# Five weight and cache loads of a two-layer decode kernel, split into DMAs of 112, 8 and 8 rows

## The chip, the cores and the metric

The kernel runs on one core of a Trainium2 chip. The metric is the device time of one execution in microseconds (us). Before the change it is 2562.59 us, the median of 3 runs (2562.34 to 2562.93).

The core has five engines with instruction streams of their own: TensorE (PE, with its weight loads as PEld), VectorE (DVE), ScalarE (ACT), GpSimd (POOL) and SyncE (SP). Here SP issues every transfer between device memory (HBM) and the on-chip memory (SBUF, 128 partitions). A transfer is carried out by up to sixteen DMA engines at once, each with a queue of its own, and each adds one to the transfer's semaphore when its part has landed.

## The reference

Two layers, each a cached attention block followed by an MLP block, for a batch of 2 and one new token. All inputs are bfloat16.

```python
def _A_ref(x, k_cache, v_cache, wq, wo):          # B=2, Sq=1, D=576, H=32, Sk=16384, Dh=128
    q = (x @ wq).reshape(B, Sq, H, Dh).transpose(0, 2, 1, 3)
    scores = jnp.einsum("bhqd,bhkd->bhqk", q, k_cache) * (Dh ** -0.5)
    p = _softmax(scores, axis=-1)
    o = jnp.einsum("bhqk,bhkd->bhqd", p, v_cache)
    return o.transpose(0, 2, 1, 3).reshape(B, Sq, H * Dh) @ wo

def _B_ref(x, w1, w2, w3, w4):                    # w1, w2: 576x576, w3: 576x4608, w4: 4608x576
    h = _gelu(_layernorm(x) @ w1)
    ...
    x1 = x + jnp.concatenate([g0, g1, g2, g3], axis=-1) @ w2    # shifted quarters of h
    return x1 + _gelu(_layernorm(x1) @ w3) @ w4

x = A_x
for _ in range(2):
    x = x + _A_ref(_layernorm(x), A_k_cache, A_v_cache, A_wq, A_wo)
    x = x + _B_ref(_layernorm(x), B_w1, B_w2, B_w3, B_w4)
```

Both layers read the same caches and weights. With 64 pairs of batch and head, one layer reads 64 K tiles and 64 V tiles of 16384x128 numbers, 4 MB each. (A few tiles at the border of the layers are kept and read once.)

## The kernel before

**Memory and order of loads.** One SBUF tensor, `mem`, has six slots of 32768 bytes in each partition. A K or V tile fills one slot: partition p holds 128 cache rows one behind another, so that a tile is a DMA of 128 rows of 32768 bytes. Weights go into parts of the same slots. `plan_all` lists every load of the whole program once, in the order of issue, with its place: `plan_tile` and `plan_piece` (L421, L429) list K and V tiles, `plan_cols` (L434) lists wq and w3, cut by 128 of their 576 rows into four loads of 128 rows and one of the 64 rows that are left (as 128 half rows), `plan_rows` lists wo and w4 (rows of 1152 bytes), and `plan_small` w1 and w2. A 128-row load of w3 has rows of 9216 bytes.

**The queue.** `Store.pump` (L286) takes the list from the front: a load is issued as soon as every cell of its place is free, and a load that has to wait holds up all that come behind it. `Graph.dma` (L91) makes one SP operation of a planned load: it may consist of several DMAs ("starts"), all of which add 16 to one semaphore, and a user waits for the sum. `release` frees a place when its last user is done.

**Compute.** `attention` (L769) goes over the 64 pairs. For each K tile, PE transposes half of it (L963), ACT copies the transposes out (L974), PE makes scores from them (L985), and DVE computes the other half of the scores by multiplying and reducing (L1007, L1011). After a softmax (L1018 to L1037) PE multiplies with the V tile (L1067). Between the layers, and at the end, come the projections: wo, two LayerNorms, w3 (`z_projection`, L736), gelu, and w4 (`rows_projection`, L715); then, for layer 1, wq. While these run, the first transposes of layer 1 are already made (`ahead`), and at the end of the kernel the same projections are followed by the store of the result.

**Names.** In both layers the loads behind the last V tile are, in the order of the queue: wo in pieces, then (layer 1 alone) w1, then w3 as five loads and w4 in pieces. In layer 0 wq of layer 1 and the rest of a K tile follow. w1 of layer 1 is a DMA of 4x128 rows, one of 56 rows and one of 8 rows.

Of the kernel before, what the change touches and what calls it, by code (L numbers as in the profile page):

```python
# [327 lines left out]
class KB:  # L328
# [89 lines left out]
        self.mps = ps("mps", [128, 512], FP32)  # L418


    def plan_tile(self, t, u, slot, cuts=()):  # L421

        b, hh = u % self.B, u // self.B
        src = (self.K if t == "k" else self.V)[b, hh].rearrange("(p j) d -> p (j d)", p=128)
        cuts = [0, *cuts, self.NB]
        for a, z in zip(cuts[:-1], cuts[1:]):
            self.plan_piece(t, u, slot, src, a, z - a)

    def plan_piece(self, t, u, slot, src, a, n):  # L429
        sem = f"tile{slot}" if n == self.NB else f"piece{slot}_{a}_{n}"  # L430
        self.store.plan((t, u, a, n), sem, slot * self.TILE + 256 * a, 256 * n,
                        [(lambda m: m, src[:, a * 128:(a + n) * 128])])

    def plan_cols(self, nm, l, w, ats):  # L434

        n = w.shape[1]
        for k in range(self.KT - 1):
            self.store.plan((nm, l, k), f"{nm}{k}", ats[k], 2 * n, [(lambda m: m, w[k * 128:(k + 1) * 128, :])])
        k = self.KT - 1
        self.store.plan((nm, l, k), f"{nm}{k}", ats[k], n,  # L440
                        [(lambda m: m, w[k * 128:, :].rearrange("r (h n) -> (r h) n", h=2))])
# [16 lines left out]
    def plan_all(self):  # L458

        T, U, n = self.TILE, self.U, self.KT - 1  # L460
        row, w3r, wqr = 2 * self.D, 2 * self.F, 2 * 128 * self.H
        self.plan_cols("wq", 0, self.wq, [4 * T + wqr * k for k in range(self.KT)])
        self.plan_small("w2", 0, self.w2, 4 * T + wqr * n + wqr // 2, (0, 64))

        tiles = self.tile_order(0)
        place = [i % 6 for i in range(len(tiles))]
        place[-2:] = [2, 4]
        third, half, Q = U - self.CARRY - 1, self.BP, self.QUARTER
        for (t, u), slot in zip(tiles, place):
            self.plan_tile(t, u, slot, {("k", third): (Q,), ("v", U - 1): (half,)}.get((t, u), ()))  # L470
        assert place[tiles.index(("k", third))] == 1

        self.cuts = {}
        up, lo = 27648, 4608
        self.cuts["wo", 0] = [(a, b, a * row) for a, b in ((0, 11), (11, 22), (22, 28), (28, 32))]
        self.cuts["w4", 0] = [(0, 3, 32 * row), (3, 7, lo), (7, 15, w3r), (15, 23, up), (23, 31, 2 * w3r),
                              (31, 35, 0), (35, 36, lo)]
        self.plan_rows("wo", 0, self.wo, self.cuts["wo", 0])
        self.plan_cols("w3", 0, self.w3, [0, w3r, 2 * w3r, up, 0])
        self.plan_rows("w4", 0, self.w4, self.cuts["w4", 0])  # L480
        self.plan_cols("wq", 1, self.wq, [T, w3r, w3r + wqr, 0, w3r + 2 * wqr])

        b, hh = third % self.B, third // self.B
        self.plan_piece("k", third, 1, self.K[b, hh].rearrange("(p j) d -> p (j d)", p=128), 0, Q)
        tiles = self.tile_order(1)
        place = [0, 3] + [(3, 0, 2, 5, 4, 1)[i % 6] for i in range(2, len(tiles))]
        for i, (t, u) in enumerate(tiles):
            self.plan_tile(t, u, place[i], (half,) if i in (0, 1, 2, 4, len(tiles) - 1) else ())
        self.cuts["wo", 1] = [(0, 11, 4 * T), (11, 22, 4 * T + 11 * row), (22, 32, 5 * T)]
        at = 5 * T + 10 * row  # L490
        w4_at = T + 2 * w3r + w3r // 2
        self.cuts["w4", 1] = [(0, 8, w4_at)] + \
                             [(a, b, 3 * T + (a - 8) * row) for a, b in ((8, 16), (16, 24), (24, 30), (30, 34), (34, 36))]
        self.plan_rows("wo", 1, self.wo, self.cuts["wo", 1])
        self.plan_small("w1", 1, self.w1, 4 * T + 22 * row, (0, 56, 64))
        self.plan_cols("w3", 1, self.w3, [at, at + w3r, T, T + w3r, T + 2 * w3r])
        self.plan_rows("w4", 1, self.w4, self.cuts["w4", 1])

    def order(self, l):
# [663 lines left out]
```

## Time and profile before

| What | Value |
|---|---|
| median of the runs | 2562.59 us |
| the profiled execution: its own time | 2563.53 us |
| the profiled execution: its span | 2561.8 us |
| busiest engine, DVE | 1913.5 us (75% of the span) |
| PE, ACT | 1614.4 us (63%), 1209.7 us (47%) |
| bytes read from HBM | 1095.26 MB, 428 GB/s over the span |
| chain that ended last | DMA 64%, DVE 25%, waiting for nothing shown 5%, PE 4% |

The profile is of one execution. Its page gives the busy time of each engine, the span in forty equal slices (each digit the busy share in tenths), the DMA queues, and the chain that ended last: followed back from the last instruction, at each step to what released it. The trace behind it answers further questions: the chain in order of time, the work in a window, the waits of a queue, and the single DMA packets and semaphore increments. "SPq" is SP's issue of a DMA; "hardware_dynamic" is the queue of the kernel's own transfers, and "instruction" queues bring the engines their programs.

### The profile page before, as it was taken

The numbers are of one execution on the slowest core, as the hardware profiler recorded it, in microseconds if no ns is written. First come the engines' busy times: TensorE is split into PE (matmuls) and PEld (weight loads), VectorE is DVE, ScalarE is ACT, GpSimd is POOL, SyncE is SP. The second block draws the span as 40 slices with busy tenths as digits, with TensorE's granted clock in tenths as the row PEclk, the third lists the DMA queues.
The fourth block names the chain that finished last, engine by engine and source line by source line (L and its number), as shares of the span: only waits on it lengthen the run. The fifth ranks groups of instructions, "written<-read, shape, count | busy, mean of one in ns | idle before, by whom it ended". The sixth has DMA issues, their size and how long they took to land.

```text
span 2561.8 us, 74731 instructions
## 1 busy us (share of the span) xinstructions
PE 1614.4 (63%) x34341; PEld 1580.3 (62%) x34341; DVE 1913.5 (75%) x2049; ACT 1209.7 (47%) x1820; POOL 51.4 (2%) x149
## 2 busy tenths in 40 slices
PE   3666566666656666666667766666666665666665
PEld 3666566666656666665657766656665665666665
DVE  5877777777777777777549987777777777777773
ACT  3544444544444444454435554444454444445442
POOL 0000000000000000000000000000000000000000
PEclk8555655555555555555555555565555555555555
DMA  9999999999999999999999999999999999999999
GB/s 408 429 431 432 432 432 431 432 432 432 431 431 432 432 432 432 432 432 431 413 403 430 430 432 432 431 431 432 432 431 432 432 432 430 432 433 432 430 432 354
DMA packets 59189, 1096.06 MB, mean 428 GB/s; under 512 B 4858, under 2 KB 23422, under 8 KB 23934
## 3 DMA queue, kind: packets, MB, share of 16 engines
q1 hardware_dynamic: 59134, 1095.28, 100.0%
q8 instruction: 40, 0.66, 0.1%
q14 instruction: 15, 0.12, 0.0%
HBM read 1095.26 MB, written 0.00 MB: 428 GB/s over the span
## 4 chain that ended last, share of the span: by engine, by line
DMA 64%; DVE 25%; issue 5%; PE 4%; SPq 1%; ACT 0%; POOLq 0%; DVEq 0%
DMA mem<-in_A_k_cache_dram 61%; DVE s_dve L1011 14%; DVE prod L1007 9%; DMA mem<-in_A_wo_dram 2%; PE tps L963 2%; SPq L101 1%; PE mps L1067 1%; DMA mem<-in_B_w_dram 1%; PE sps L934 1%; DMA mem<-in_A_wq_dram 0%; PE sps L985 0%; DVE diag L930 0%; DVE q_col L927 0%; DVE mx L1020 0%; DVE l L1048 0%
## 5 line engine op out<-in xcount | busy, mean ns | idle before, releaser
L974 ACT ACTIVATE kt<-tps 128x1024 bf16<-128x1024 bf16 x1028 | 1039.9, 1024 | 901.8 <-PE tps L963 883.9
L1011 DVE TENSOR_REDUCE s_dve<-prod 128x16 f32<-128x2048 bf16 x512 | 1166.2, 2278 | 17.6
L963 PE MATMUL tps<-ident,mem 128*128 128x128 bf16 x8224 | 1004.9, 300 | 143.9 <-POOLq L202 138.7
L1007 DVE TENSOR_TENSOR prod<-mem,qb 128x2048 bf16<-128x2048 bf16 x512 | 624.5, 1220 | 520.4 <-POOLq L202 486.3
L963 PEld LDWEIGHTS tps<-ident,mem 128*128 128x128 bf16 x8224 | 766.2, 136 | 153.9 <-POOLq L202 148.3
L1067 PE MATMUL mps<-p,mem 128*128 128x1 bf16 x16384 | 512.0, 165 | 543.4 <-POOLq L202 510.7
L1067 PEld LDWEIGHTS mps<-p,mem 128*128 128x128 bf16 x16384 | 487.6, 104 | 551.5 <-ACT p L1037 544.1
L985 PEld LDWEIGHTS sps<-q_col,kt 128*128 128x128 bf16 x8224 | 412.5, 113 | 10.1 <-ACT kt L974 9.5
L985 PE MATMUL sps<-q_col,kt 128*128 128x1 bf16 x8224 | 401.0, 170 | 8.6 <-ACT kt L974 8.0
L934 PE MATMUL sps<-diag,ones_bf 128*128 128x128 bf16 x129 | 37.1, 288 | 195.1 <-DVE diag L930 195.1
L934 PEld LDWEIGHTS sps<-diag,ones_bf 128*128 128x128 bf16 x129 | 13.5, 105 | 205.6 <-DVE diag L930 205.5
L1032 ACT ACTIVATE mx<-mx 128x1 f32<-128x1 f32 x128 | 26.0, 203 | 230.6 <-POOL mx L1024 230.6
L937 ACT ACTIVATE qb<-sps 128x128 bf16<-128x128 f32 x129 | 35.8, 277 | 140.4 <-PE sps L934 140.4
L1024 POOL PARTITION_ALL_REDUCE mx<-mx x128 | 49.2, 385 | 2455.2 <-DVE mx L1022 2406.8
L1034 ACT ACTIVATE p<-s_dve,mx 128x64 bf16<-128x64 f32 x128 | 44.5, 347 | 4.1
L1037 ACT ACTIVATE p<-sps,mx 128x64 bf16<-128x64 f32 x128 | 37.6, 294 | 0.0
L1020 DVE TENSOR_REDUCE mx<-sps 128x1 f32<-128x64 f32 x128 | 27.5, 215 | 6.1 <-PE sps L985 6.1
L930 DVE TENSOR_SCALAR diag<-ident,q_f 128x128 bf16<-128x128 bf16 x129 | 31.6, 245 | 0.0
L728 PE MATMUL mps<-prod,mem 128*128 128x2 bf16 x680 | 21.1, 166 | 15.5 <-DMA mem<-in_B_w_dram 8.3
L728 PEld LDWEIGHTS mps<-prod,mem 128*128 128x128 bf16 x680 | 19.8, 104 | 17.0 <-DMA mem<-in_B_w_dram 9.0
L708 DVE TENSOR_TENSOR x<-x,mps 128x8 f32<-128x8 f32 x4 | 0.7, 163 | 35.3 <-PE mps L728 35.3
L1018 DVE TENSOR_REDUCE mx<-s_dve 128x1 f32<-128x64 f32 x128 | 26.6, 208 | 0.0
(91 smaller groups left out, 224.3 us busy)
## 6 DMA issues: line engine op xcount, KB each, us to landing
mem<-in_A_v_cache_dram SPq DMA_DIRECT2D x123, 4096.0 KB, 49.6
mem<-in_A_k_cache_dram SPq DMA_DIRECT2D x121, 4096.0 KB, 40.7
mem<-in_B_w_dram SPq DMA_DIRECT2D x14, 1152.0 KB, 11.2
mem<-in_A_v_cache_dram SPq DMA_DIRECT2D x6, 2048.0 KB, 20.8
mem<-in_A_k_cache_dram SPq DMA_DIRECT2D x6, 2048.0 KB, 12.4
mem<-in_A_wq_dram SPq DMA_DIRECT2D x8, 1024.0 KB, 8.1
mem<-in_A_wo_dram SPq DMA_DIRECT2D x4, 1584.0 KB, 26.8
mem<-in_B_w_dram SPq DMA_DIRECT2D x7, 576.0 KB, 9.8
```

Source lines behind the costliest of these rows:

```text
L728: ins = pe.matmul(self.mps[:, t * B:(t + 1) * B], lhsT=buf[:, o:o + 128], rhs=rhs(k), start=(k == 0 and t == 0), stop=(k == last), skip_gr ...
L934: self.pe(lambda pe: pe.matmul(qps, lhsT=self.ones_bf[:, :], rhs=self.diag[:, :], start=True, stop=True, skip_group_check=True), reads=["o ...
L937: self.act(lambda e: e.activation(out=self.qb[i][:, :], in_=qps, func=ACT.Copy), reads=[("qps", i)], writes=[("qb", i)], sig=("qb", i))
L963: ins = pe.transpose(self.tps[t][:, j * 128:(j + 1) * 128], buf[:, j * 128:(j + 1) * 128], self.ident[:, :])
L974: self.act(lambda e: e.activation(out=self.kt[k][:, :, :], in_=self.tps[t][:, :].rearrange("p (i c) -> p i c", i=self.CH), func=ACT.Copy), ...
L985: ins = pe.matmul(self.sps[sp][:, c * self.CH + j:c * self.CH + j + 1], lhsT=self.kt[k][:, j, :], rhs=self.q_col[:, sp:sp + 1], start=True ...
L1007: self.dv(lambda e: e.tensor_tensor(out=prod, in0=buf.rearrange("p (j d) -> p j d", d=128), in1=qbc, op=ALU.mult), reads=[("qb", r)] + key ...
L1011: self.dv(lambda e: e.tensor_reduce(out=sd[:, c0:c0 + DB], in_=prod, axis=AX.X, op=ALU.add), reads=["prod"], writes=[("s_dve", r)], sig=(" ...
L1024: self.pool(lambda e: e.partition_all_reduce(mx[3], mx[2], channels=128, reduce_op=ROP.max), reads=[("mx2", i)], writes=[("mx3", i)])
L1034: self.act(lambda e: e.activation(out=p[:, n:self.NB], in_=self.s_dve[i][:, 0:self.NB - n], func=ACT.Exp, bias=mx[4], scale=self.scale, ac ...
L1037: self.act(lambda e: e.activation(out=p[:, 0:n], in_=self.sps[i][:, 0:n], func=ACT.Exp, bias=mx[4], scale=self.scale, accum_out=self.ls[:, ...
L1067: ins = pe.matmul(self.mps[:, 448:449], lhsT=buf[:, j * 128:(j + 1) * 128], rhs=p[:, col:col + 1], start=(h == 0 and b == 0), stop=(h == 1 ...
```

## The change

Five loads of 128 rows become three DMAs each: rows 0 to 111, 112 to 119 and 120 to 127. They are the first K tile of layer 0 and the w3 loads 0 and 2 of each layer. The places, the order of the loads and the bytes stay as they are; a changed load's semaphore now counts 48 in place of 16. The title in the source of the change: nine rows for each of eight DMA engines and seven for the others.

```diff
-    def plan_tile(self, t, u, slot, cuts=()):
+    def plan_tile(self, t, u, slot, cuts=(), lean=False):
...
-            self.plan_piece(t, u, slot, src, a, z - a)
+            self.plan_piece(t, u, slot, src, a, z - a, lean)
-    def plan_piece(self, t, u, slot, src, a, n):
+    def plan_piece(self, t, u, slot, src, a, n, lean=False):
...
-                        [(lambda m: m, src[:, a * 128:(a + n) * 128])])
+                        self.rows_of(lambda m: m, src[:, a * 128:(a + n) * 128], lean))
+    @staticmethod
+    def rows_of(f, src, lean):
+
+        rows = (0, 112, 120, 128) if lean else (0, 128)
+        return [(lambda m, a=a, b=b: f(m)[a:b], src[a:b]) for a, b in zip(rows[:-1], rows[1:])]
-    def plan_cols(self, nm, l, w, ats):
+    def plan_cols(self, nm, l, w, ats, lean=()):
...
-            self.store.plan((nm, l, k), f"{nm}{k}", ats[k], 2 * n, [(lambda m: m, w[k * 128:(k + 1) * 128, :])])
+            self.store.plan((nm, l, k), f"{nm}{k}", ats[k], 2 * n,
+                            self.rows_of(lambda m: m, w[k * 128:(k + 1) * 128, :], k in lean))
...
-            self.plan_tile(t, u, slot, {("k", third): (Q,), ("v", U - 1): (half,)}.get((t, u), ()))
+            self.plan_tile(t, u, slot, {("k", third): (Q,), ("v", U - 1): (half,)}.get((t, u), ()),
+                           lean=(t, u) == ("k", 0))
...
-        self.plan_cols("w3", 0, self.w3, [0, w3r, 2 * w3r, up, 0])
+        self.plan_cols("w3", 0, self.w3, [0, w3r, 2 * w3r, up, 0], lean=(0, 2))
...
-        self.plan_cols("w3", 1, self.w3, [at, at + w3r, T, T + w3r, T + 2 * w3r])
+        self.plan_cols("w3", 1, self.w3, [at, at + w3r, T, T + w3r, T + 2 * w3r], lean=(0, 2))
```

## The prediction

> **What bounds the kernel now.** I read the page's slices first, then its queue table, then the chain of waits near the end and around the change of layer.
>
> ```profile
> DMA  9999999999999999999999999999999999999999
> GB/s 408 429 431 432 432 432 431 432 432 432 431 431 432 432 432 432 432 432 431 413 403 430 430 432 432 431 431 432 432 431 432 432 432 430 432 433 432 430 432 354
> q1 hardware_dynamic: 59134, 1095.28, 100.0%
> q8 instruction: 40, 0.66, 0.1%
> q14 instruction: 15, 0.12, 0.0%
> ```
>
> The sixteen DMA engines are busy in every slice, and the rate stands at 432 GB/s except at the start, around 1240 to 1340 us and at the end. No compute engine is over 75%. So the time is the queue time of the DMA engine that finishes last, plus the gaps in which that engine waits. The last three lines are the other point: the same engines also fetch instructions, 40 blocks of 16 KB and some of 8 KB, unevenly.
>
> ```profile
> 2515.38 14.29 DMA mem<-in_A_wo_dram
> ...
> 2547.13 2.22 SPq L101
> 2549.39 7.97 DMA mem<-in_B_w_dram
> 2557.40 0.44 PE mps L728 x10
> ```
>
> The chain of waits of the last 50 us (start, length, what): the end hangs on transfers and on SP's issues, which are held up because the queue is full; the last w4 piece lands at 2557.36 and only 4.4 us of work follow. In the window table (busy times, clock, DMA share, GB/s) the hand-over between the layers runs at 388 GB/s with DMA still full, and only the last stretch drains:
>
> ```profile
> 1270.00:1320.00 50.00, 27.74 (x678) 25.27 (x677) 11.62 (x59) 11.96 (x16) 0.00 (x0) 0.50 1.02 388
> 2530.00:2562.00 32.00, 15.26 (x426) 13.83 (x423) 8.55 (x50) 5.22 (x8) 0.00 (x0) 0.50 0.81 309
> ```
>
> **The engines one by one.** The trace holds, for each transfer, the times of its sixteen semaphore increments, one for each engine, and the start, length and size of each packet. They show how far the engines are apart (us after the first to finish):
>
> ```
> V tile landing from 1230.89   0 .14 .15 .86 1.14 1.36 1.57 1.63 1.64 1.75 1.77 1.84 2.86 3.06 3.25 3.29
> V tile landing from 2473.10   0 .10 .16 .49 .61 1.10 1.10 1.38 2.07 2.44 2.82 3.10 3.37 3.60 3.70 5.50
> last w4 piece, from 2553.88   0 .01 .07 .24 .42 .43 .45 1.00 1.37 1.56 1.60 1.70 2.05 2.29 2.69 3.48
> ```
>
> The order hardly changes inside a layer, since every engine has the same rows to move and none runs dry. A transfer counts as landed with its last engine, so the kernel runs at the latest one: at the end 2.27 us behind the mean (2555.09). Following the packets back to back from 18 to 132 us shows whence it comes: a 16 KB fetch delays its engine by 1.55 us (one engine lands at 25.95 and then at 37.21, where 9.71 is the period). The fetches go round eight engines only: those at 1347.6, 1355.0 and 1362.9 us hit the engines that those at 1411.0, 1419.6 and 1527.2 hit, eight fetches later. At 123 us the eight that fetched are 1.4 to 1.9 behind, two of them 3.2 and 3.4; of the others six are 0 to 1.1 and two, which read the 8 KB blocks, 2.0 and 2.95.
>
> Which eight? The w1 load of layer 1 tells, since its last 64 rows come as 56 and 8. An engine with a share of both shows two extra end marks (4-byte packets), one with a share of the 56 alone shows one, the last two show none. So I can sort the engines where w3 starts (2527.24 us): the eight that took the 8 rows are 0, .01, .04, .06, .28, .53, .56 and 1.24 behind (mean 0.34), the others .44, .53, .86, 1.51, 1.75, 1.77, 1.91 and 3.71 (mean 1.56). The eight with the extra rows are the early ones, and the latest engine of all is not among them. That the late eight are the fetching eight is inferred: their number, and seven of the latest eight, agree. [...]
>
> **The change part by part.** No arithmetic, byte or buffer changes; each of five loads becomes three DMAs, ten more in all.
>
> Rows moved. A 32 KB row costs its engine 9.713/8 = 1.21 us (tile period of the steady stretch), a 9216-byte row 2.776/8 = 0.347 us (w3 loads landing at 2533.39 and 2536.17). The late eight lose 1.21 (first K tile) and twice 0.35 (w3) in layer 0 and twice 0.35 in layer 1: 1.21 + 0.69 + 0.69 = 2.6 us. The early eight gain as much. Layer 1's 0.69 arrives at the end in full: w3 to w4 run as one full queue there, and 3.71 - 0.69 = 3.02 is still over 1.24 + 0.69 = 1.93, so the same engine stays last.
>
> Layer 0's 1.9 us has to pass the hand-over, whose chain (first column start, second length) is
>
> ```profile
> 1243.52 28.11 DMA mem<-in_A_wo_dram
> ...
> 1283.84 6.61 DMA mem<-in_B_w_dram
> ...
> 1293.26 10.15 DMA mem<-in_B_w_dram
> ...
> 1304.68 10.65 DMA mem<-in_A_wq_dram
> ```
>
> Each of these ends with its latest engine. At the wo loads the fetching engines come down from 3.29 to 2.1, but the early side goes up by 1.21, and the engine of the 8 KB blocks (2.86, by my sorting on that side) to 4.07: wo lands 0.8 later. At the last w3 (1290.44) its latest engine, a fetching one, is earlier by 1.21 + 0.69 = 1.9, while the 8 KB engine, at about 1288.3 now, comes to 1290.2: a gain of 0.2. At the last w4 (1303.85) the latest has just had a fetch (1294.3); it drops to 1301.9, the 8 KB engine stands at 1302.1: a gain of 1.7. The wq loads start when w4 is consumed and gain 1.4 or so (first engine now 1312.15 against last 1313.76 for the fourth, and the start of wq, held by gelu, gains only the 0.2). So layer 1 begins some 1.4 us sooner for engines that wait there (they idle about 0.4 us at 1315.5), and the latest, which never waits, is 1.9 ahead. At the end the latest engine is 2.6 earlier, 2554.8; engines that waited at the hand-over gain 1.4 + 0.7 if late-sided (2556.57 becomes 2554.5) and 1.4 - 0.7 if early-sided (about 2555.4, the 8 KB engine, becomes 2554.7). That leaves 2.3 to 2.6 with everything fitting; I take 2.2.
>
> Added issues. An 8-row DMA holds SP 0.30 us (the 8-row w1 piece), a free 128-row one 0.33 to 0.43. Ten are 3 to 4 us of SP's time, but beside full queues: k0's two stand at 5.6 us, when the engines have work until 16; in the hand-over SP waits between the w3 issues anyway (1269.26, then 1274.57), and the third pair moves an issue from 1276.75 to 1277.5, needed at 1282; in layer 1 the issues of 2525.5 to 2528.6 are needed from 2530.2 on, and the one behind them stands 11.99 us on a full queue. So I cost them at 0; without cover it would be +4. The end mark that each added DMA puts on eight engines takes 9 ns, under 0.05 us in all. The first K tile may land 0.4 us later (two engines without a 16 KB fetch land at 27.3, then at 28.5; the last is at 28.12 now); PE and DVE start on it later and then wait for transfers anyway (40.7 us of each 58.3 in the chain are a transfer), so it costs nothing.
>
> The profiled execution took 2563.53, its span 2561.8; the median of the runs is 2562.59, 0.94 below. Span: 2561.8 - 2.2 = 2559.6, execution 2561.3, median 2560.4.
>
> [...]
>
> **Rivals.**
> *Hand-over keeps layer 0's share.* If wo's 0.8 delay moves the LayerNorm chain, w3's consumption and wq's issue, layer 1 starts where it did, and engines of the late side that wait there gain 0.69 alone: 2561.9. For it: the chain passes that stage. Against: w4 and wq are held by fetching engines.
> *Overcorrection, the slower case.* The 8 KB engine is 1.21 + 0.69 later in layer 0 and stays last through the hand-over; it decides if it sits over 2.0 behind before w3. Layer 1 then starts 0.8 to 1.5 later, less 0.69 at the end: up to +0.8, 2563.4. Against: now it falls to under 1 by 1301.
> *Sides swapped.* If the extra rows land on the late eight, the latest gains 2.6: 2565.2. Against: the end marks in w1.
> *A fixed price per small DMA*, a gap behind each of the ten. The nearest row is the two-row load of x on empty queues, issued at 0.79 and landed at 2.16: 1.4 us each gives 2562.6 + 14 = 2576.6. [...]
> *More than the rows*: evener engines also let SP's full-queue stalls end sooner, -5 or beyond: 2557.
>
> **Chances.** Forecast 0.55 (alone 2559.4 to 2561.4), hand-over 0.22, overcorrection 0.12, sides swapped 0.05, fixed price 0.03, more 0.03. The range 2559.3 to 2563.4 takes in the first three with their price bounds. A change of 0.2% (5.1 us, about what a measurement of this kernel tells from none) is beyond all but the last two: faster 0.03, slower 0.04 (with a little of the swap), same 0.93.
>
> **What would show it.** Right: the first K tile's packets nine and seven to an engine; the increments of the last w4 piece within about 2.2 us instead of 3.48, the last at 2555; the last wq landing near 1314. Wrong: wq landing at or after 1315.3 (hand-over), the last increments coming from engines with nine rows (overcorrection), a spread over 4 us at the end (swap), idle engines behind an 8-row DMA (fixed price).

## The result, and the profile after

The kernel became slower: 2599.14 us (median of 4 runs, 2597.12 to 2600.97) against 2562.76 us (median of 4 runs, 2562.34 to 2563.18), a ratio of 1.0142 (95% interval 1.0130 to 1.0154), 36.4 us. The profiled execution took 2597.12 us, the least of the four; its span is 2595.4 us. The stages below are read from the two profiled executions, which differ by 33.6 us.

The busy times of PE, DVE and ACT are those of before (1612.8, 1913.7 and 1209.9 us), and so are the bytes. The page's slices of the changed kernel show where the time went:

```profile
DMA  9999999999999999999999999999999999999999
GB/s 322 426 432 432 431 433 430 433 431 432 432 431 433 430 434 429 434 431 431 384 366 429 432 430 433 430 433 431 433 431 432 431 431 433 431 433 431 433 429 289
q1 hardware_dynamic: 59214, 1095.28, 99.9%
```

The DMA engines are still busy in every slice, but they move less: 322 GB/s for 408 in the first slice, 384 and 366 for 413 and 403 in the middle, 289 for 354 in the last. These are the places of the five changed loads. The steady stretches between them run at 432 GB/s as before. So the engines hardly wait for an issue; the packets themselves take longer. The packet records say how long: between 17 and 28 us a row of 32 KB takes 2.0 us in the median, between 30 and 40 us, where the 8-row parts run, 4.6 us (up to 5.2). Before, the median was 1.22 us.

The chain of waits of the kernel before at its start (start, length, what):

```profile
5.04 23.08 DMA mem<-in_A_k_cache_dram
```

The chain of the changed kernel from its start, around the hand-over, and at the end; pieces under 0.1 us are left out where no dots stand:

```profile
5.62 1.64 SPq L101
7.31 36.50 DMA mem<-in_A_k_cache_dram
43.91 1.24 DVE prod L1015
...
1280.48 11.95 DMA mem<-in_A_wo_dram
...
1300.29 13.11 DMA mem<-in_B_w_dram
...
1316.08 10.27 DMA mem<-in_B_w_dram
...
1327.63 11.08 DMA mem<-in_A_wq_dram
...
2537.09 15.37 DMA mem<-in_A_wo_dram
...
2573.74 3.56 SPq L101
2577.34 3.00 SPq L101
2580.38 2.39 SPq L101
2582.81 8.14 DMA mem<-in_B_w_dram
```

The first K tile holds the chain for 36.5 us, from 7.31 to 43.81; before, it landed at 28.12 (5.04 + 23.08). The second K tile lands with its first engine at 47.70 us (35.94 before) and with its last at 53.21 (37.84). At the hand-over the issue of layer 1's first K half slips from 1314.85 to 1338.52 us, and the last w4 piece lands at 2590.95 instead of 2557.36. So the start costs some 12 to 15 us, the w3 loads of layer 0 about 10, those of layer 1 about 10. Two windows of the changed kernel (window, length, busy times with counts, PE clock, DMA share, GB/s) cover the last two:

```profile
1270.00:1345.00 75.00, 40.80 (x1041) 37.34 (x1040) 18.40 (x72) 15.56 (x25) 0.35 (x1) 0.50 1.01 337
2530.00:2596.00 66.00, 30.37 (x848) 28.21 (x845) 15.38 (x67) 10.79 (x18) 0.35 (x1) 0.50 0.91 287
```

DMA shares of 1.01 and 0.91 at 337 and 287 GB/s: busy and slow again.

### The profile page after: what moved, and what is told of

Read it like the earlier page. It is cut to its first block, busy times and chain, and to the rows that moved or that the text cites. A ratio compares the mean times of both kernels' runs of the same rounds, so it can differ in the third digit from the quotient of the medians.

```text
span 2595.4 us, 74741 instructions
## 1 busy us (share of the span) xinstructions
PE 1612.8 (62%) x34341; PEld 1578.5 (61%) x34341; DVE 1913.7 (74%) x2049; ACT 1209.9 (47%) x1820; POOL 51.4 (2%) x149
## 3 DMA queue, kind: packets, MB, share of 16 engines
q1 hardware_dynamic: 59214, 1095.28, 99.9%
## 4 chain that ended last, share of the span: by engine, by line
DMA 63%; DVE 25%; issue 5%; PE 4%; SPq 3%; ACT 0%; POOLq 0%; DVEq 0%
DMA mem<-in_A_k_cache_dram 61%; DVE s_dve L1019 13%; DVE prod L1015 9%; SPq L101 3%; PE tps L971 1%; PE mps L1075 1%; DMA mem<-in_B_w_dram 1%; DMA mem<-in_A_wo_dram 1%; PE sps L942 1%; DMA mem<-in_A_wq_dram 0%; PE sps L993 0%; DVE diag L938 0%; DVE mx L1028 0%; DVE q_col L935 0%; DVE l L1056 0%
## 5 line engine op out<-in xcount | busy, mean ns | idle before, releaser
L665 PE MATMUL sps<-xn,mem 128*128 128x2 bf16 x544 | 16.5, 165 | 26.0 <-DMA mem<-in_B_w_dram 21.9
L736 PEld LDWEIGHTS mps<-prod,mem 128*128 128x128 bf16 x680 | 19.7, 104 | 20.3 <-DMA mem<-in_B_w_dram 9.2
L665 PEld LDWEIGHTS sps<-xn,mem 128*128 128x128 bf16 x544 | 15.5, 104 | 26.8 <-DMA mem<-in_B_w_dram 22.5
```

What stands on the lines that cost most here:

```text
L736: ins = pe.matmul(self.mps[:, t * B:(t + 1) * B], lhsT=buf[:, o:o + 128], rhs=rhs(k), start=(k == 0 and t == 0), stop=(k == last), skip_gr ...
```

## The experiments

Four theories stood against each other. **P, partitions:** which partitions are written at the same moment sets how long a row takes. **U:** the uneven split itself is the loss. **F:** a price for each small DMA. **S, source:** rows that lie together in device memory are slow to read for several engines at once. Later N joined them: the number of engines at work explains it all.

No trace here names the engine or the partition of a packet; what the runs show is how long the packets take. By what the engines disturb each other was not shown.

All changes are to the kernel before, if nothing else is said.

**e1, the K tile's split alone**

```diff
  (the changed kernel)
-        self.plan_cols("w3", 0, self.w3, [0, w3r, 2 * w3r, up, 0], lean=(0, 2))
+        self.plan_cols("w3", 0, self.w3, [0, w3r, 2 * w3r, up, 0])
-        self.plan_cols("w3", 1, self.w3, [at, at + w3r, T, T + w3r, T + 2 * w3r], lean=(0, 2))
+        self.plan_cols("w3", 1, self.w3, [at, at + w3r, T, T + w3r, T + 2 * w3r])
```

> Of the change only the split of the first K tile. [...] Theory F (a fixed price of 1.4 us per added DMA): two DMAs, 2565.5. Theory U (nine and seven rows are themselves the loss): 1.2 us at most, 2564.

Measured: 2577.05 us against 2563.21, ratio 1.0053 (1.0030 to 1.0076), +13.8 us. F would allow 2.8 and U 1.2. The trace of the whole change has 12 to 15 for this load (the second K tile, above), so e1 shows that this split alone costs it, and not yet why.

**e2, the four w3 loads alone**

```diff
  (the changed kernel)
-                           lean=(t, u) == ("k", 0))
+                           lean=False)
```

> Of the change only the four w3 loads. P: about 5 us for each load, since the 9216-byte packets of the 8-row parts stretch as those of the K tile do; 36 less the 12 to 15 of the K tile, so 2583 to 2587 us. F: eight added DMAs of 1.4 us, 2574. If the two parts don't add up to the whole 36 us, they hide each other.

Measured: 2583.53 us against 2563.21, ratio 1.0079 (1.0049 to 1.0108), +20.3 us, 5.1 for each load. With e1's 13.8 it makes 34.1 of the 36.4: the parts add up. Where the five w3 loads of layer 1 run, the window of the kernel before and that of e2 read (columns as above):

```profile
2527.00:2540.00 13.00, 5.58 (x151) 5.07 (x149) 3.58 (x24) 1.87 (x3) 0.00 (x0) 0.50 1.03 417
```

```profile
2535.00:2557.00 22.00, 5.83 (x149) 5.15 (x146) 3.58 (x24) 1.87 (x3) 0.00 (x0) 0.50 1.04 236
```

The same work takes 22 us in place of 13, at 236 GB/s. The 9216-byte packets of this window take 0.67 us in the median for 0.35, and nine in ten of all that belong to these loads take 0.48 us or more; half of them are of the loads 1 and 3, which were not split. So rows of whole loads are slowed too while a split load is under way.

**e3, no unevenness: 112 and 16 rows**

```diff
+            starts = [(lambda m, x=x, y=y: m[x:y], rows[x:y]) for x, y in ((0, 112), (112, 128))]
```

(`rows` is the source of the first K tile, `starts` the DMAs of its load; the same names stand in the edits below.)

> The first K tile as 112 rows and 16 rows: every engine has eight rows, as before the change. U: no loss, 2562.7 us. F: one added DMA, 2564.2. [...]

Measured: 2573.45 us against 2563.21, ratio 1.0039 (1.0023 to 1.0055), +10.2 us. With eight rows meant for every engine, most of the loss stays, so U falls. The last rows (29 to 34 us) take 4.1 us in the median; the 112-row part takes 2.03 us a row in the median (17 to 28 us). Rows that start at the same moment have nearly the same length, 1.95 to 2.3 us between 17 and 21 us, and mostly 1.4 to 1.5 us around 24 us. How the 112 rows are dealt to the engines stays open.

**e4, all engines, twice 64 rows**

```diff
+            starts = [(lambda m, x=x, y=y: m[x:y], rows[x:y]) for x, y in ((0, 64), (64, 128))]
```

> The first K tile as twice 64 rows, four rows for each engine in each, all sixteen engines. U: no loss, 2562.7 us. F: 2564.2. [...]

Measured: 2574.60 us against 2563.21, ratio 1.0045 (1.0025 to 1.0064), +11.4 us; a row takes 2.56 us (2.34 to 2.70, between 17 and 29 us), twice the usual 1.22. Sixteen engines at work (DMA share 0.99), nothing uneven, one DMA more, and each row takes twice as long. The window from 16 to 46 us (columns as above; the kernel before moves 428 GB/s there, its line stands under e5 to e8):

```profile
16.00:46.00 30.00, 11.81 (x268) 11.44 (x268) 7.92 (x10) 6.77 (x9) 0.00 (x0) 1.00 0.99 266
```

**e5 to e8, source against destination.** The first K tile as 16 DMAs of 8 rows. An 8-row DMA is carried out by eight engines: with ten of them added, the queue has 59214 packets for 59134 (q1, above and in the prediction), eight end marks for each. That it is the same eight every time is inferred; e9, below, shows two groups of eight. "Near" is eight neighbours, "step" eight rows or partitions that are four apart.

```diff
+            near = [slice(8 * i, 8 * i + 8) for i in range(16)]
+            step = [slice(32 * i + j, 32 * i + j + 29, 4) for i in range(4) for j in range(4)]
+            to, fr = near, near          # e5;  e6: step, step;  e7: near, step;  e8: step, near
+            starts = [(lambda m, x=x: m[x], rows[y]) for x, y in zip(to, fr)]
```

> The first K tile as 16 DMAs of 8 neighbouring rows into 8 neighbouring partitions, all on eight engines (16 rows each). Eight engines alone, each at 1.21 us a row, would cost 9.7 us: 2572 us (theory N: nothing but the number of engines). [...] F: 15 added DMAs of 1.4 us, 2572 + 21 = 2593.

> The same 16 DMAs of 8 rows on the same eight engines, but each takes every fourth row and writes every fourth partition. [...] F: 2593.

> As before in DMAs, engines and bytes, but every fourth row of the source goes to neighbouring partitions, so that rows of this K tile lie in other partitions than their V rows and the output differs. [...]

> Neighbouring rows of the source go to every fourth partition (rows of this K tile lie in other partitions than their V rows, the output differs). [...]

Measured, one run each, against 2563.33 us for the kernel before on the same chip:

| partitions written | source rows near | source rows four apart |
|---|---|---|
| near | e5: 2634.89 (+71.6) | e7: 2629.52 (+66.2) |
| four apart | e8: 2583.18 (+19.9) | e6: 2583.83 (+20.5) |

The rows of the table differ by 46 to 52 us, its columns by 1 to 5. By P the table's rows should differ, by S its columns: the destination decides, not the source; S falls, and so does F, since all four have the same sixteen DMAs. Each of the four is a single run, but the repeated runs of one kernel here lie within 4 us of each other. The window from 16 to 46 us of the kernel before, of the changed one, of e5, e7 and e8, in this order:

```profile
16.00:46.00 30.00, 14.32 (x313) 13.61 (x314) 18.11 (x18) 9.97 (x13) 0.00 (x0) 0.87 1.01 428
```

```profile
16.00:46.00 30.00, 7.20 (x192) 6.93 (x193) 3.36 (x8) 2.18 (x5) 0.00 (x0) 1.00 0.98 232
```

```profile
16.00:46.00 30.00, 5.10 (x172) 4.82 (x172) 1.41 (x7) 1.30 (x3) 0.00 (x0) 1.00 1.02 125
```

```profile
16.00:46.00 30.00, 5.10 (x172) 4.82 (x172) 2.19 (x12) 2.06 (x4) 0.00 (x0) 1.00 1.04 133
```

```profile
16.00:46.00 30.00, 5.09 (x172) 4.82 (x172) 1.62 (x8) 1.55 (x3) 0.00 (x0) 1.00 1.01 270
```

The last two columns tell it: the engines' share is about 1 in all five, while the rate is 428, 232, 125, 133 and 270 GB/s. A row takes 4.3 us in e5 and 4.1 in e7 (medians of this window), and 5.4 and 5.1 us between 50 and 90 us; the rate of e5 falls further:

```profile
46.00:76.00 30.00, 0.00 (x0) 0.00 (x0) 0.00 (x0) 0.00 (x0) 0.00 (x0) 1.00 0.98 96
```

These are 3.5 and 4.5 times 1.21 in e5; why it goes in two steps is not shown.

e6 and e8 also speak against N: the eight engines have 9.7 us more work, yet the kernel loses 20. The packets show where: in e6 the median row takes 1.21 us from 18 to 25 us and 2.55 us from 30 to 42 us, and in e8 too. That the engines that skip the tile have by then run ahead into the next one, and that this slows the rows of both, is inferred.

The slowing also reaches engines that take no part in the split load. In e5 112 rows start between 16 and 46 us, and each takes 3.8 us or more. The eight engines of the small DMAs can have made at most about 64 of them, so the others belong to the eight engines that are in the next tile, a whole load of 128 partitions, and none of those rows goes at 1.21 us either. So what slows the split load slows all sixteen engines alike here. What ties the engines together stays open; the even slowing in e3 and that of the whole w3 loads in e2 look like the same.

**e10, farther apart**

```diff
+            starts = [(lambda m, j=j: m[j:j + 113:16], rows[j:j + 113:16]) for j in range(16)]
```

> The 16 DMAs of 8 rows once more, now into partitions sixteen apart (source rows sixteen apart too), farther from each other than in the fast case of four apart. Theory Q (engines disturb each other when their partitions are close): as fast as four apart or faster, 2583 us or less, packets of 1.21 us. [...]

Measured, one run: 2608.94 us against 2562.51, +46.4 us; packets of 3.6 us in the median. The window from 16 to 46 us:

```profile
16.00:46.00 30.00, 4.99 (x172) 4.71 (x171) 1.30 (x6) 1.03 (x3) 0.00 (x0) 1.00 1.05 157
```

Partitions that are sixteen apart disturb each other more than those four apart (+46.4 for +20.5 us), so nearness alone isn't what counts, and theory Q falls. By what rule partitions disturb each other is not shown; measured are the patterns of e5 (+71.6 us), e10 and e6. Here too all rows are slow, whatever load they belong to (3.1 to 3.7 us from 18 to 68 us).

**e9, the aim of the change without its neighbouring partitions**

```diff
+            c = 14336
+            to = [slice(32 * i + j, 32 * i + j + 29, 4) for j in range(4) for i in (0, 2, 1, 3)]
+            starts = [(lambda m: m[:, 0:c], rows[:, 0:c])] + \
+                     [(lambda m, x=x: m[x, c:], rows[x, c:]) for x in to]
```

> The aim of the change without its neighbouring partitions: the first K tile's rows without their last 4 KB as one DMA of 128 rows, and the last 4 KB of all rows as 16 DMAs of 8 rows, four partitions apart, on the eight engines that are early. In bytes an engine has nine rows' worth or seven, as in the change. If engines alone set the rate (theory N, the sum of the prediction), the late eight come to the next tile 1.2 us sooner and the early eight 1.2 later, and the kernel gains up to 1.2 us: 2561.5 to 2562.7. [...]

Measured: 2565.82 us (11 runs) against 2562.67 (15), ratio 1.0013 (1.0004 to 1.0022), +3.2 us; N, which had a gain, falls. The semaphore increments of the second K tile show the two groups (us after 35.94, the first engine of the kernel before):

```
before   0    .11  .22  .30  .32  .32  .34  .35  .36  .38  .46  .50  1.06 1.12 1.71 1.90
e9       .21  .24  .25  .31  .43  .45  .75  1.82 2.89 2.91 2.93 3.00 3.18 3.24 3.25 4.00
```

By N eight engines were to come 1.2 us sooner and eight 1.2 later. Eight come as before and eight about 2.6 us later (2.9 to 3.0 for 0.35 in the middle of the row). So an engine that hands rows over gained nothing here, and packets were slower meanwhile: between 24 and 29 us, while the 4 KB parts are written, these take about 0.23 us for 0.16 before, and the 32 KB rows of the other engines 1.5 to 1.9 us for 1.22. So e9 isn't free of conflicts either, and a way of handing rows over that has none was not tried.

None of these versions beats the kernel before.

## Why the prediction was wrong

It forecast 2560.4 us, within 2559.3 to 2563.4; 2599.14 came.

- **What bounds the kernel** was right: the DMA engines are busy throughout, and what the loads took longer came out at the end, 34 of 36 us as a plain sum of e1 and e2.
- **The failing step is "Rows moved. A 32 KB row costs its engine 9.713/8 = 1.21 us".** That figure is from loads of 128 partitions, and the sum carried it over to loads of 112 and 8. Measured: 2.0 us in the 112-row part and 4.6 in the 8-row parts (0.67 for 0.35 in the w3 group). The first term, 1.21 us gained, became a loss of 13.8 (e1); the four w3 rows, 1.4 us gained, became 20.3 lost (e2). No run shows row by row the nine and seven from which the sum took these terms; the traces show eight end marks for each added DMA, and in e9 two groups of eight engines, neither of which came sooner.
- **The gain itself did not come in e9 either.** It avoids neighbouring partitions and was to give nine rows' worth and seven; eight engines came as before and eight about 2.6 us later. What the prediction called an engine's work depends on which partitions are written meanwhile, by all engines (+71.6 us in e5, +20.5 in e6).
- **The rivals** included none in which the rows themselves take longer. One sign misled: wq landing after 1315.3 us was to speak for the hand-over, and it landed at 1338.71 us because the loads before it were slow. The slower ones were priced from rows that have nothing to do with it: 2563.4 (overcorrection), 2565.2 (sides swapped) and 2576.6 (a fixed price). The last had the sign, but e5 to e8 have sixteen DMAs each and differ by up to 52 us, so there is no price per DMA of that size.
- **What I looked at** was the gap between packets, 10 ns in the kernel before, and not their length: e4, with two halves of 64 rows, has rows of 2.56 us for 1.22 and lost 11.4 us.
- **The added issues** cost nothing that shows: engines had work throughout (share 0.98 to 1.01 in the first and middle windows).
- **The 56 and 8 rows of w1**, from which I read which engines take 8 rows, said nothing on the price: they are only 64 rows of 1152 bytes, behind 512 others of that size.
- **The hand-over, the 8 KB engine, and how much of layer 0 would pass** were not tested by these runs: the conflicts covered them. The sixteen engines end no closer together: the last w4 piece lands over 3.66 us (2587.29 to 2590.95), 3.48 before, where the prediction had about 2.2. That fetches of instructions make the engines uneven (1.55 us for 16 KB) stands as it was inferred from the trace; that moving rows mends it was not borne out.

## What to carry to other kernels

Before splitting a load by rows, ask which partitions will be written at the same moment: loads of 128 partitions ran here at 1.22 us for a row of 32 KB, those of 112 and 64 neighbouring partitions at 2.0 and 2.6 us, and those of 16 and 8 at 4.1 us and more, all in the median. Price a new shape of transfer by a run, or by a row of that very shape, and not by the time per row of another; a busy DMA engine at half the GB/s is the sign of it (232 GB/s for 428 here, at a share of 0.98). In e9, rows given to other engines brought the engines that gave them nothing, so evening out engines this way isn't to be counted on where every load fills all partitions.

## What was not expected of the hardware

- Partitions sixteen apart (+46.4 us) conflict more than partitions four apart (+20.5 us), with the same engines, DMAs and bytes.
- The split loads slowed all sixteen engines, also those that took no part in them: in e5 no row that starts between 16 and 46 us takes less than 3.8 us, and in e2 most rows of the w3 loads that were not split are slow as well.
- The 112-row part slows all its engines together, to about 2.0 us a row with a dip to about 1.4 around 24 us (e3); why stays open.
- In the kernel before, the fetch of a 16 KB block of instructions delays one DMA engine by 1.55 us (it lands at 25.95 and then at 37.21 us, where 9.71 is the period). That these fetches go round eight of the sixteen is inferred.
